# Two DMAs of 64 partitions for one spread row of inverses, in a banded attention with a two-layer network

## The chip, the cores and the metric

The kernel runs on one core of a Trainium2 chip. The metric is device microseconds of one execution, and the median of several runs is compared. The profile is of one execution of its own, whose time stands beside its span below.

## The reference

Banded attention is computed for 8 batches, 8 heads, 576 positions and head dimension 64: each position sees itself and the 63 before it. Its output, 4608 rows of 512, goes through two matrices with a leaky rectifier between them. All is float32.

```python
scores = scale * np.matmul(q, k.transpose(0, 1, 3, 2))
mask = (rel >= 0) & (rel < window)
scores = np.where(mask, scores, -1000000000.0)
scores = scores - np.max(scores, axis=-1, keepdims=True)
attn = np.exp(scores)
attn = attn / (np.sum(attn, axis=-1, keepdims=True) + 1e-09)
out = np.matmul(attn, v)
...
h = x @ w_in
g = np.maximum(0.01 * h, h)
return g @ w_out
```

## The kernel before

**Main work.** The 4608 rows are nine chunks of 512. Chunks 0 to 2 go directly through both matrices: tiles `h` (L431, L919) are the first product and `acc` (L467, L928) the second, each number split into a high and a low part and multiplied three times. Chunks 3 to 8 go two at a time in three passes, in which seven products take the place of eight: `m` (L1117) for the first matrix in all three, `z` (L1180) for the second in the last two; the first pass takes the plain products `y` (L1137) for it. The sums around the products `m` are on VectorE (L1126) and the rectifier on ScalarE (L1129). The weight pieces come through a ring of four tiles that GpSimd fills by DMA (L1101). Pieces of weights that are summed for the seven products are prepared on VectorE and ScalarE (L1032 to L1048) and stored by ScalarE's queue.

**Attention.** It is done in 36 pairs of blocks of 64 queries, ahead of the main work that needs their rows. The first eight pairs, with the main work beside them, follow a list written by hand (`ORDER`). From pair 8 on, a pair m takes these steps, which the change touches in part:

- scores on TensorE (L278), scale and mask on VectorE (L666), from pair 20 on a copy on ScalarE (L672)
- maximum over the keys, which lie on the partitions, on GpSimd (L681), subtraction on VectorE (L688), exponential on ScalarE (L692)
- sum over the keys on GpSimd (L684) into `late_o`, one of two tiles; all partitions hold the same row of 512 sums, one row for each half j of the heads
- compaction: SyncE issues a DMA of one partition's 512 sums to 64 partitions of 8 (L695, `late_c`, one of two tiles); small adds and inverses then take 8 numbers a partition (L699 on ScalarE, L703 on VectorE)
- row store: a DMA of the 1024 inverses to a row of `rows` in device memory (L716)
- spread: a DMA that reads this row back into `late_r` (L728), where partitions 0 to 63 all hold the first 512 numbers and partitions 64 to 127 the other 512. There is one `late_r`, so the spread of a pair waits for the product of the pair before
- values on TensorE (L740), in pairs 8 to 19 a copy on ScalarE (L747, tile `late_n`), and the product with `late_r` on VectorE (L752)
- keep: the result goes to `x_rows` in device memory (L755), and four fetches a pass (L867) bring it back, after which VectorE and ScalarE build the operands of the products `m` (L874, L893, L896)

Pair 19 multiplies by whole sums without compaction and spread, so 27 pairs of the 28 have a spread.

**What sets the order.** From pair 8 on every step is an entry of a plan (`op`, L532), with its engine, its expected duration, the entries that it waits for, a rank, and for DMAs a time to landing. `arrange` (L544) walks the plan as a list scheduler: it takes the engine that can begin first, on it the entry of the lowest rank that is ready, and lets at most eight DMAs of SyncE and ScalarE be under way. Every engine then issues its entries in that order and no other; the waits between engines are semaphores. `load` (L537) makes an entry of SyncE's queue, with a landing time of 4.8 us if none is given; compaction, row store, spread and keep are such entries. The fetch is given 5.0.

Of the kernel before, what the change touches and what calls it, by code (L numbers as in the profile page):

```python
# [104 lines left out]
def band_attention_ffn(ctx: ExitStack, tc: tile.TileContext, qk, vW, vL, w_in, w_out, eye_mask, out, outT):  # L105
    nc = tc.nc
# [298 lines left out]
    later = {}  # L405
# [118 lines left out]
    order, late = ORDER.split("|")  # L524
# [7 lines left out]
    def op(engine, us, fn, *after, rank=1.0, lag=0.12, land=0.0):  # L532
        x = dict(engine=engine, us=us, fn=fn, after=[a for a in after if a], rank=rank, lag=lag, land=land, n=len(plan))
        plan.append(x)
        return x

    def load(fn, *after, rank=1.0, us=0.5, land=4.8):  # L537
        return op("SP", us, fn, *after, rank=rank, land=land)

    def bulk(fn, *after, rank=1.0, land=6.5):  # L540
# [53 lines left out]
    def x_all(k):  # L594
        n = X_FIRST if k < X_FIRST else 7 - X_FIRST
        t = hold("xb", F32R, 2) if k < X_FIRST else hold("few", F32R, FEW)
        return t.rearrange("p (k i c) -> p k i c", k=n, i=2), k - X_FIRST * (k >= X_FIRST)
# [23 lines left out]
    rows = dram.tile([NU // 2, 1024], F32, name="rows")  # L621
# [13 lines left out]
    for name in late.split():  # L635
        kind = name.rstrip("0123456789")
        n = int(name[len(kind) :])
        o = weights_of.setdefault(n, {})
        if kind == "raw":
            o["raw"] = op("ACT", 0.45, partial(fetch_w, n), weights_of.get(n - 3, {}).get("join"), rank=0.2, lag=1.5, land=6.0)  # L640
            continue
        engine, us = ("ACT", ACTS) if kind in ("abs", "chi") else ("DVE", ONE)
        before = {
            "bits": ["raw"], "sign": ["bits"], "abs": ["sign"], "clamp": ["abs"], "join": ["clamp"], "chi": ["join"],
            "rest": ["chi"],
        }[kind]
# [58 lines left out]
    def direct(m):  # L705
        return DIRECT_FROM <= m < EARLY
# [17 lines left out]
    def by_unit(x):  # L724
        return x.rearrange("p (w k c) -> p k w c", k=NP, w=UNITS)

    def spread_of(m):
        nc.sync.dma_start(later["r"], rows[m].rearrange("(j c) -> j c", j=2)[:, None].broadcast_to([2, 64, 512]))  # L728

    def early(m):  # L730
        return m < EARLY
# [37 lines left out]
    at, summing = {}, []  # L769
# [37 lines left out]
    def normalise(m):  # L807

        late = 0.0 if early(m) else 0.45
        soon = 0.15 if early(m) and m > 13 else 0.8 + late  # L810
        o, before, two, after = at[m], at.get(m - 1, {}), at.get(m - 2, {}), at.get(min(m + 2, EARLY - 1))
        if "v" in o and before:
            o["v"]["after"] += [x["V"] for x in (two,) if x]
        if direct(m):
            spread = o["I"] = op("DVE", 4.4, partial(whole_inverse_of, m), o["c0"], o["c1"], rank=soon)
            finish_of(m, [spread], late, soon)
            return
        guard = op("ACT", 0.22, partial(guard_of, m), o["c0"], o["c1"], rank=soon, lag=0.3 + 6 * late)
        o["I"] = op("DVE", 0.25, partial(inverse_of, m), guard, rank=min(0.4 + late, soon))
        o["rows"] = load(partial(rows_of, m), o["I"], rank=0.3 + late)  # L820
        for j in range(2):
            if m + 2 in at and not direct(m + 2):
                at[m + 2][f"c{j}"]["after"].append(o["rows"])
        spread = [load(partial(spread_of, m), o["rows"], before.get("Y"), rank=0.3 + late)]
        finish_of(m, spread, late, soon)

    def finish_of(m, spread, late, soon):
        o, before, two, after = at[m], at.get(m - 1, {}), at.get(m - 2, {}), at.get(min(m + 2, EARLY - 1))
        if early(m):
            free = [after["E1"], before.get("take"), o["A0"] if direct(m) else o["I"]]  # L830
        else:
            free = [both_free if early(m - 2) else two["Y"]]
        o["V"] = op("PE", 1.0, partial(values_of, m), o.get("v"), o["X0"], o["X1"], *free, before.get("V"), rank=0.5 + late, lag=LAG if early(m) else 2 * LAG)
        kept = two.get("kept", [])
        if early(m):
            o["take"] = op("ACT", ACTS, partial(take_of, m), o["V"], *kept, rank=0.5 + late)
        o["Y"] = op("DVE", TWO if early(m) else ONE, partial(product_of, m), *spread, o.get("take"), o["V"], *kept, rank=soon, lag=0.3 + 6 * late)
        for x in summing if direct(m) else ():
            x["after"].append(o["Y"])
        if m < UPC // UNITS * LEAD:  # L840
            hi = op("ACT", ACTS, partial(high_early, m), o["Y"], *x2_free, rank=soon)
            o["kept"] = [op("DVE", TWO, partial(low_early, m), hi, rank=soon)]
            x2.extend(o["kept"])
        else:
            o["kept"] = [load(partial(keep_of, m), o["Y"], rank=0.35 + late)]

# [3 lines left out]
    def x_build(s, n, xt_of, xt_free, x_free):  # L852

        urge, wait = ((0.2, 0.2), (1.4, 2.6), (0.6, 2.6))[s]
        m = (UPC * LEAD + 2 * UPC * s) // UNITS + 2 * n

        def raw():
            return xt_of()[0].rearrange("p (i q c) -> p i q c", i=2, q=4)

        def sums():  # L860
            return xt_of()[1].rearrange("p (k i c) -> p k i c", k=4, i=2)

        def part(q):
            return raw()[:, :, q] if q < 4 else sums()[:, q - 4]

        def fetch():
            nc.sync.dma_start(  # L867
                xt_of()[0].rearrange("p (i c) -> p i c", i=2), x_rows[m : m + 2].rearrange("i p c -> p i c")
            )

        got = [load(fetch, *at[m]["kept"], *at[m + 1]["kept"], *xt_free, rank=urge, land=5.0)]

        def sub(to, a, b):
            nc.vector.tensor_tensor(part(to), part(a), part(b), ALU.subtract)  # L874

        d = op("DVE", 0.5, partial(sub, 4, 0, 2), *got, rank=urge, lag=wait)
        d3 = op("DVE", 0.5, partial(sub, 6, 1, 0), *got, rank=urge, lag=wait)
        d2 = op("DVE", 0.5, partial(sub, 5, 1, 4), d, rank=urge)
        d4 = op("DVE", 0.5, partial(sub, 7, 3, 5), d2, rank=urge)

        def x_view(i, a, b):
            t, k = x_all(a)
            t = t.rearrange("p k i (n c) -> p k i n c", n=4)[:, k : k + b - a, i, n]
            return t.rearrange("p k (i c) -> p k i c", i=2)

        def source(a, b):
            if a < 3:
                return raw()[:, :, 1 + a : 1 + b].rearrange("p i k c -> p k i c")
            return sums()[:, a - 3 : b - 3]

        done = []
        for a, b, after in ((0, 2, got), (2, 3, got), (3, 7, [d, d2, d3, d4])):
            hi = op("ACT", 0.2 + 0.213 * (b - a), lambda a=a, b=b: nc.scalar.copy(x_view(0, a, b), source(a, b)), *after, *x_free, rank=urge, lag=wait)  # L893

            def low(a=a, b=b):
                nc.vector.tensor_tensor(x_view(1, a, b), source(a, b), x_view(0, a, b).bitcast(F32), ALU.subtract)  # L896

            done.append(op("DVE", 0.2 + 0.35 * (b - a), low, hi, rank=urge))
        return done
# [179 lines left out]
    x_free, xt_free = [x for f in range(5) for x in slot_free[f]] + evicted[1], [slot_free[12], slot_free[13]]  # L1079
    x_done = []  # L1080
    for n in range(4):
        xt_free[n % 2] = x_build(0, n, partial(halves_of, XT_AT + n % 2), xt_free[n % 2], x_free)
        x_done += xt_free[n % 2]
# [19 lines left out]
    def filled(of, *after):  # L1103
        n = next(fills)
        return n, op("POOL", 0.6, partial(fill, n, of), *tile_free[n % RING], *after, rank=0.2, land=7.0)
# [97 lines left out]
    def second_in_seven(s):  # L1203
# [70 lines left out]
        if s < NS - 1:  # L1274
            x_done[:] = []
            last_of = {}
            for n in range(4):
                last_of[n % 2] = x_build(s + 1, n, partial(xt_late, n), [*quiet[1], *quiet[2], *last_of.get(n % 2, [])], [x_used])
                x_done.extend(last_of[n % 2])
# [7 lines left out]
    for s in range(NS):  # L1287
        for f in range(half):
# [4 lines left out]
            for k in range(7):  # L1293
                p, b = 7 * f + k, bank_at(s, BANK[k])
                if p % 4 == 0:
                    made_before = [] if s else [y for x in range(f, min(f + 2, half)) for y in prepared[0, x]]
                    n, got = filled(w_first[:, 512 * p : 512 * (p + 4)], *made_before)
                after = bank_free[b] if k < 4 else reads[b]
# [31 lines left out]
        for t in range(2):  # L1330
            for f in range(FT):
                if f % 2 == 0:
                    q = next(pair_of)
                    j, p = f // half, f % half // 2
# [5 lines left out]
                if f % 2 == 0:  # L1340
                    n, got = filled(w_second[:, f : f + 2])
                for i in range(4):
                    after = bank_free[i] if f == 0 else ()
# [9 lines left out]
        if s < NS - 1:  # L1353
            x_done, last_of = [], {}
            for n in range(4):
                tile = 2 * (n % 2)
                free = [split_of[0, f + i * half] for f in (tile, tile + 1) for i in range(2)] + last_of.get(n % 2, [])
                last_of[n % 2] = x_build(s + 1, n, partial(halves_of, tile), free, [x_used])
                x_done += last_of[n % 2]
# [67 lines left out]
```

## Time and profile before

| | before |
|---|---|
| median of 3 runs | 960.24 us (958.60 to 962.86) |
| the profiled execution, its own time | 958.28 us |
| its span, first to last instruction | 956.5 us |
| mean granted TensorE clock | 0.96 |
| TensorE matmul busy | 873.3 us |
| VectorE, ScalarE, GpSimd busy | 609.5, 374.7, 365.3 us |
| DMA traffic | 226.79 MB, mean 237 GB/s |

An instruction's row names its line, engine, operation, output and inputs. In the view of waits a row says which engine, with which tile and line, waited for what: microseconds in total, times, the longest. In the timeline and the chain a row begins with its start and its duration; a bracket gives the idle time ahead of an instruction and what ended it. The view of windows gives for each stretch the busy time of TensorE's matmuls, its weight loads, VectorE, ScalarE and GpSimd with the number of instructions, then the granted clock, the mean busy share of the 16 DMA engines, and GB/s. "SPq" is SyncE's queue, which issues DMAs. A 128x512 matmul group of 336 takes 76.16 us at clock 1.00.

### The profile page before, as it was taken

How to read it: one execution, taken by the hardware profiler on the slowest of the kernel's cores; microseconds unless marked ns; L12 is line 12 of the kernel's file. 1: busy time of each engine (PE TensorE's matmuls, PEld its weight loads, DVE VectorE, ACT ScalarE, POOL GpSimd, SP SyncE). 2: the span in 40 equal slices, each digit the busy share in tenths (PEclk: the TensorE clock that was granted, in tenths of full speed). 3: DMA queues.
4: the chain of work that ended last, by engine and by line, in shares of the span. 5: the costliest groups of instructions: out<-in, count | busy, mean ns of one | idle time of the engine just before them, and what ended most of it. 6: DMA issues, size and time to landing. Idle time of an engine off the chain costs nothing.

```text
span 956.5 us, 16749 instructions
## 1 busy us (share of the span) xinstructions
PE 873.3 (91%) x6778; PEld 704.5 (74%) x6778; DVE 609.5 (64%) x883; ACT 374.7 (39%) x605; POOL 365.3 (38%) x218
## 2 busy tenths in 40 slices
PE   9999999998888799986968799977899999999998
PEld 6877888877767578764857676755688888888886
DVE  7999867455445768554644859537467984455763
ACT  5666553323222344332422324323245442333442
POOL 5321006776756416564736646744011111011110
PEclk9999999999998899997989899978999999999999
DMA  9776758875777669876859697974888787656772
GB/s 331 236 229 191 220 170 269 249 275 190 287 225 252 204 228 327 279 248 204 297 178 350 201 351 256 303 234 136 281 273 225 231 230 227 206 185 185 211 209 99
DMA packets 98531, 226.79 MB, mean 237 GB/s; under 512 B 14743, under 2 KB 45591, under 8 KB 88983
## 3 DMA queue, kind: packets, MB, share of 16 engines
q0 software_dynamic: 23136, 90.18, 30.6%
q10 hardware_dynamic: 35664, 77.31, 24.6%
q1 hardware_dynamic: 39654, 58.24, 18.1%
q8 instruction: 53, 0.87, 0.4%
q14 instruction: 24, 0.19, 0.1%
HBM read 172.52 MB, written 53.06 MB: 236 GB/s over the span
## 4 chain that ended last, share of the span: by engine, by line
PE 49%; DMA 33%; DVE 11%; issue 3%; POOL 2%; ACT 1%; SPq 1%; ACTq 0%; DVEq 0%; POOLq 0%
PE z L1180 16%; PE m L1117 13%; DMA late_r<-rows 12%; DMA late_c<-late_o 7%; PE acc L928 4%; PE h L919 4%; PE h L431 4%; PE acc L467 4%; DMA rows<-late_c 3%; DMA w_second<-p 3%; DMA w_sums<-pspare 2%; PE s L278 1%; DMA w_single<-w 1%; POOL late_o L684 1%; DMA pxb<-sum 1%
## 5 line engine op out<-in xcount | busy, mean ns | idle before, releaser
L1117 PE MATMUL m<-pfew,p 128*128 128x512 f32 x720 | 177.8, 403 | 13.4 <-DVE p L1126 11.2
L1117 PEld LDWEIGHTS m<-pfew,p 128*128 128x128 f32 x720 | 138.9, 195 | 45.2 <-DVE p L1126 12.1
L928 PE MATMUL acc<-p,gs 128*128 128x512 f32 x324 | 81.6, 399 | 0.0
L1129 ACT ACTIVATE p<-p 128x512 f32<-128x512 f32 x60 | 37.8, 631 | 98.5 <-DVE p L1126 98.3
L681 POOL PARTITION_ALL_REDUCE g<-late_f x20 | 38.2, 1938 | 98.9 <-DVE late_f L666 71.3
L1117 PE MATMUL m<-pxb,p 128*128 128x512 f32 x288 | 71.9, 397 | 3.7 <-ACT p L1129 3.4
L1101 POOL DMA_DIRECT2D p<-w_first x42 | 22.7, 541 | 133.5 <-PE m L1117 88.8
L684 POOL PARTITION_ALL_REDUCE late_o<-late_f x20 | 65.0, 3280 | 21.7 <-ACT late_f L692 19.0
L684 POOL PARTITION_ALL_REDUCE late_o<-late_e x18 | 59.8, 3336 | 32.5 <-DMA late_c<-late_o 22.8
L684 POOL PARTITION_ALL_REDUCE late_o<-e x18 | 58.9, 3293 | 33.9 <-ACT e L692 15.5
L928 PEld LDWEIGHTS acc<-p,gs 128*128 128x128 f32 x324 | 60.6, 190 | 13.0
L1126 DVE TENSOR_TENSOR p<-m,pxa 128x512 f32<-128x512 f32 x60 | 41.3, 689 | 41.6 <-PE m L1117 41.3
L1117 PEld LDWEIGHTS m<-pxb,p 128*128 128x128 f32 x288 | 54.5, 191 | 16.4 <-ACT p L1129 3.8
L1137 PE MATMUL y<-gs,p 128*128 128x512 f32 x192 | 50.6, 412 | 12.5 <-DVE p L1126 8.0
L1126 DVE TENSOR_TENSOR pxa<-m,pxa 128x512 f32<-128x512 f32 x60 | 41.3, 688 | 31.1 <-PE m L1117 25.9
L752 DVE TENSOR_TENSOR late_n<-o,late_r 128x512 f32<-128x512 f32 x16 | 10.9, 682 | 76.1 <-DMA late_r<-rows 76.1
L919 PE MATMUL h<-pxa,p 128*128 128x512 f32 x228 | 55.6, 394 | 3.6 <-DVE gs L939 3.6
L1180 PE MATMUL z<-gs,p 128*128 128x512 f32 x240 | 57.7, 390 | 0.0
L1137 PEld LDWEIGHTS y<-gs,p 128*128 128x128 f32 x192 | 37.0, 198 | 22.2 <-DVE p L1126 8.1
L919 PEld LDWEIGHTS h<-pxa,p 128*128 128x128 f32 x228 | 42.9, 190 | 13.8 <-DVE gs L939 4.8
L1180 PEld LDWEIGHTS z<-gs,p 128*128 128x128 f32 x240 | 45.1, 188 | 9.3
L1180 PE MATMUL z<-third,p 128*128 128x512 f32 x216 | 51.9, 390 | 0.0
(191 smaller groups left out, 1778.2 us busy)
## 6 DMA issues: line engine op xcount, KB each, us to landing
p<-w_first POOLq DMA_DIRECT2D x42, 1024.0 KB, 6.8
p<-w_second POOLq DMA_DIRECT2D x28, 1024.0 KB, 7.7
p<-w_sums POOLq DMA_DIRECT2D x16, 1024.0 KB, 5.1
qk<-qk ACTq DMA_DIRECT2D x26, 512.0 KB
pspare<-w_second ACTq DMA_DIRECT2D x16, 512.0 KB
w_sums<-pspare ACTq DMA_DIRECT2D x16, 512.0 KB
raw<-w_out ACTq DMA_DIRECT2D x15, 512.0 KB
raw<-w_in ACTq DMA_DIRECT2D x14, 512.0 KB
```

The lines of the kernel that those rows point to most:

```text
L431: nc.tensor.matmul(ps, a[:, k, :], b[:, k, part], start=n == 0, stop=n == len(terms) - 1)
L467: nc.tensor.matmul(acc[c, i], a[:, ts], b, start=begin and n == 0, stop=end and n == 2)
L681: nc.gpsimd.partition_all_reduce(most_of(j), e_of(m)[:, j], P, ReduceOp.max)
L684: nc.gpsimd.partition_all_reduce(sum_of(j), e_of(m)[:, j], P, ReduceOp.add)
L919: nc.tensor.matmul(ps, a[:, k, :], b[:, k], start=i == 0, stop=i == len(terms) - 1)
L928: nc.tensor.matmul(acc[c, i], a[:, i * P : (i + 1) * P], b, start=begin and k == 0, stop=n in ends and k == 2)
L1101: nc.gpsimd.dma_start(to, of)
L1117: nc.tensor.matmul(tiles[b], w[:, 256 * i + 128 * kt : 256 * i + 128 * kt + 128], x_part(OF_X[k], j, kt), start=begin and c == 0, stop=c = ...
L1126: nc.vector.tensor_tensor(to(), tiles[b], x(), ALU.add)
L1129: nc.scalar.activation(to(), to() if b is None else tiles[b], AF.Prelu, alpha=0.01)
L1137: nc.tensor.matmul(tiles[i], a, b, start=f == 0 and k == 0, stop=f == FT - 1 and k == 2)
L1180: nc.tensor.matmul(tiles[b + i], a, x, start=begin and f == 0 and c == 0, stop=f == half - 1 and c == 2, skip_group_check=not begin,)
```

## The change

The spread becomes two DMAs, one for each 64 partitions, each of which repeats 512 numbers 64 times. The source of the one before had the two halves as its first size and 64 repeats as its second. Three landing times of the plan are other numbers, and the ordered list is made anew from the plan; nothing of the arithmetic changes.

```diff
-    def load(fn, *after, rank=1.0, us=0.5, land=4.8):
+    def load(fn, *after, rank=1.0, us=0.5, land=5.0):
...
-    def spread_of(m):
-        nc.sync.dma_start(later["r"], rows[m].rearrange("(j c) -> j c", j=2)[:, None].broadcast_to([2, 64, 512]))
+    def spread_of(m, j):
+        nc.sync.dma_start(later["r"][64 * j : 64 * j + 64], rows[m, 512 * j : 512 * j + 512][None].broadcast_to([64, 512]))
...
-        spread = [load(partial(spread_of, m), o["rows"], before.get("Y"), rank=0.3 + late)]
+        spread = [load(partial(spread_of, m, j), o["rows"], before.get("Y"), rank=0.3 + late) for j in range(2)]
...
-            o["kept"] = [load(partial(keep_of, m), o["Y"], rank=0.35 + late)]
+            o["kept"] = [load(partial(keep_of, m), o["Y"], rank=0.35 + late, land=6.0)]
...
-        got = [load(fetch, *at[m]["kept"], *at[m + 1]["kept"], *xt_free, rank=urge, land=5.0)]
+        got = [load(fetch, *at[m]["kept"], *at[m + 1]["kept"], *xt_free, rank=urge, land=6.5)]
```

SyncE's queue, in the products `y` of the first pass (in the trace before, this piece begins at 554.68 us). `late_r<-rows` is the spread, `outT` an output store, `x_rows<-late_n` the keep, `late_c<-late_o` a compaction, `rows<-late_c` a row store, `p<-x_rows` a fetch. Before:

```order
L728 DMA late_r<-rows 128x1x512
L1195 DMA outT<-p_25_3083 128x512 x2
L1195 DMA outT<-p_24_2950 128x512 x2
L755 DMA x_rows<-late_n 128x512
L695 DMA late_c_1771<-late_o_1769 64x1x8
L716 DMA rows<-late_c_1772 128x8
L867 DMA p_37_4002<-x_rows 128x2x512
L695 DMA late_c_1771<-late_o_1770 64x1x8
L728 DMA late_r<-rows 128x1x512
```

And in the changed kernel:

```order
L728 DMA late_r<-rows 64x512 x2
L867 DMA p_36_3803<-x_rows 128x2x512
L1195 DMA outT<-p_25_3089 128x512 x2
L1195 DMA outT<-p_24_2972 128x512 x2
L695 DMA late_c_1772<-late_o_1769 64x1x8
L716 DMA rows<-late_c_1771 128x8
L755 DMA x_rows<-late_n 128x512
L695 DMA late_c_1772<-late_o_1770 64x1x8
L728 DMA late_r<-rows 64x512 x2
```

Two spreads stand where one stood, and the row store L716 of the next pair, which had stood behind the keep L755 of this one, now stands ahead of it.

TensorE's queue, in the products `m` of the second pass, around the values of the last pair (`o<-late_f,more_v`, L740). Each row of six matmuls is one of the seven products of a group, and `m_3_2` is a tile of group 3; a group has four tiles, three of which take two products. Before:

```order
L1117 MATMUL m_3_0_5988<-pxb_3408,p_32_3607 128x512 x6
L1117 MATMUL m_3_1_5998<-pfew_3418,p_32_3607 128x512 x6
L1117 MATMUL m_3_2_6007<-pfew_3418,p_32_3607 128x512 x6
L740 MATMUL o_6017<-late_f,more_v 64x64 x16
L1117 MATMUL m_3_3_6036<-pfew_3418,p_29_3487 128x512 x6
L1117 MATMUL m_3_0_5988<-pfew_3418,p_29_3487 128x512 x6
```

And in the changed kernel:

```order
L1117 MATMUL m_3_3_6033<-pxb_3413,p_29_3490 128x512 x6
L1117 MATMUL m_4_0_6072<-pxb_3413,p_30_3529 128x512 x6
L1117 MATMUL m_4_1_6083<-pfew_3422,p_30_3529 128x512 x6
L740 MATMUL o_6094<-late_f,more_v 64x64 x16
L1117 MATMUL m_4_2_6113<-pfew_3422,p_30_3529 128x512 x6
L1117 MATMUL m_4_3_6125<-pfew_3422,p_30_3529 128x512 x6
```

The values of the last pair stood between the third and the fourth product of group 3, and now stand between the second and the third of group 4, six products of six matmuls later.

## The prediction

> **What bounds the kernel now.** The page comes first.
>
> ```profile
> PE 873.3 (91%) x6778; PEld 704.5 (74%) x6778; DVE 609.5 (64%) x883; ACT 374.7 (39%) x605; POOL 365.3 (38%) x218
> ```
>
> TensorE is the busy engine, but a share over the whole span hides stages. The view of windows, cut where the work changes, gives for each stretch its length, the busy time of each engine, the granted clock, the DMA share and GB/s:
>
> ```profile
> 173.00:337.00 164.00, 143.47 (x1430) 114.53 (x1431) 86.24 (x126) 52.23 (x98) 99.31 (x40) 0.94 0.71 236
> 337.00:409.00 72.00, 67.38 (x582) 54.52 (x581) 48.35 (x72) 29.79 (x52) 32.99 (x20) 1.00 0.82 276
> 409.00:693.00 284.00, 233.45 (x2012) 186.21 (x2012) 166.11 (x218) 93.23 (x154) 152.65 (x87) 0.90 0.78 255
> 693.00:956.50 263.50, 259.43 (x1144) 214.29 (x1142) 168.31 (x196) 104.25 (x133) 27.81 (x44) 1.00 0.70 208
> ```
>
> The last stage is full: 259.43 of 263.50 us busy at clock 1.00. The loss lies in the stretches where attention pairs run beside the main products. In 409 to 693 TensorE idles 284.00 - 233.45 = 50.6 us, and what it does runs at a mean clock of 0.90. As a rough estimate of its work at full clock I take 233.45 x 0.90 = 210 us, so this stage loses 74 us. By the same sum 173 to 337 holds 143.47 x 0.94 = 135 us of work and loses 29 us, and 337 to 409 loses under 5.
>
> Next, who TensorE waits for; first in 409 to 693 (total, times, longest):
>
> ```profile
> PE o L740 <- DVE late_n L752: 15.2, 3, 7.7
> PE m L1117 <- DVE p L1126: 11.5, 3, 9.1
> PE y L1137 <- DVE p L1126: 8.0, 1, 8.0
> PE o L740 <- DMA more_v<-vL: 7.8, 1, 7.8
> ```
>
> L752 is the product of a pair with `late_r`, the spread row of inverses. L1126 is an ordinary sum of the main work. Why should that be late? The timeline around 450 us shows it (start, duration, idle before and its releaser):
>
> ```profile
> 449.75 0.69 DVE L752 TENSOR_TENSOR late_n<-o,late_r 128x512 f32<-128x512 f32 x1 [11.77 <-DMA late_r<-rows]
> 450.03 0.21 ACT L699 ACTIVATE late_c<-late_c 128x8 f32<-128x8 f32 x1 [11.39 <-DMA late_c<-late_o]
> 450.20 3.23 POOL L684 PARTITION_ALL_REDUCE late_o<-e  x1 [9.49 <-DMA late_c<-late_o]
> 450.36 0.68 DVE L1126 TENSOR_TENSOR p<-m,pxa 128x512 f32<-128x512 f32 x1
> ...
> 451.09 1.22 PE L1117 MATMUL m<-pfew,p 128*128 128x512 f32 x2 [9.05 <-DVE p L1126]
> ```
>
> VectorE stands at L752 for 11.77 us, the sum L1126 queues behind it, and TensorE waits 9.05 us for a sum that has nothing to do with attention. ScalarE and GpSimd stand in the same microsecond for `late_c<-late_o`, a transfer of 2 KB issued just after the spread. How fast is the spread? The chain of waits in 409 to 693, its first and last such piece of six (start, duration):
>
> ```profile
> 412.70 15.54 DMA late_r<-rows
> ...
> 632.51 17.74 DMA late_r<-rows
> ```
>
> The six sum to 104.8 us, 17.5 each, for 256 KB. What the DMA engines do meanwhile, by windows, in the tail of one spread and in a busy stretch:
>
> ```profile
> 445.00:449.00 4.00, 0.00 (x0) 0.00 (x0) 0.00 (x0) 0.00 (x0) 0.00 (x0) 0.66 0.16 58
> ...
> 560.00:570.00 10.00, 10.00 (x98) 7.99 (x98) 4.30 (x4) 1.23 (x3) 7.38 (x3) 0.88 1.05 353
> ```
>
> From 445 to 449 no compute engine works at all, and the DMA share is 0.16: 0.16 x 16 is about 2.6 engines, where the other stretch fills all 16. So the spread trickles through two or three engines, with the others empty.
>
> This is also a loop. There is one `late_r`, so the spread of pair m waits for the product of pair m-1. One turn is the spread 17.5, its product 0.69 and the issue 0.54, or 18.7 us; 15 products lie in the 284 us, one each 18.9. The stage runs at the pace of the spread. TensorE's 210 us of work would need one in 14.0.
>
> **The change, part by part.** *The transfer.* Its source had two as its first size; each half now has 64, its partitions, on both sides. That the engines used follow the first size is my reading of the 0.16; no row of this trace varies that size alone. The Trainium skill, page "DMA: Bandwidth & Descriptors", section "Rules for kernel authors", says that an outermost size below 16, a broadcast of few copies above all, confines a DMA to at most that many engines; the 0.16 agrees. By that rule the halves go over all engines, and the sum below stays as it is.
>
> What do the two halves take together? No row shows this read over all engines, so I bound it by the nearest: large loads (KB each, median us to landing), and one 256 KB transfer of the chain that shared its queue with a slow spread.
>
> ```profile
> p<-w_first POOLq DMA_DIRECT2D x42, 1024.0 KB, 6.8
> p<-w_second POOLq DMA_DIRECT2D x28, 1024.0 KB, 7.7
> p<-w_sums POOLq DMA_DIRECT2D x16, 1024.0 KB, 5.1
> ```
>
> ```profile
> 301.14 11.69 DMA x_rows<-late_n
> ```
>
> So 5.1 us, or somewhat less, since those move four times the bytes, up to 11.7. I take 6, next to the loads. A turn of the loop is then 6 + 0.69 + two issues of 0.54, about 7.8 us, and even at 11.7 it is 13.5, under the 14.0 that TensorE needs. The loop stops being the bound in either case.
>
> *The added issues.* SyncE issues 27 more transfers:
>
> ```profile
> L728 SPq DMA_DIRECT2D late_r<-rows x27: 526/541/613, 173.8 to 690.4; - x27
> SPq L755 <- DVE late_n L752: 98.8, 12, 17.1
> ```
>
> 27 x 0.54 = 14.6 us on a queue that stood 98.8 us in 409 to 693 alone, waiting at L755 for that product. While it stands there the next row store, compactions and spread are queued behind it. This wait hides the issues; without that cover they cost 15 x 0.54 = 8 us in the loop.
>
> *The list made anew.* The three landing figures are the planner's (spread, compaction and row store 5.0, keep 6.0, fetch 6.5) and move instructions on all engines. What they move at the places above: SyncE issues a row store ahead of the keep that waits for a product where it had it behind, and the values of the last pair stand six products of six matmuls later. The first takes a wait out of the pair's chain; the second gives each pair more TensorE time. Against a faster transfer I cost both at nothing beyond what is kept back below: what they could cost is the time of a stall that stays.
>
> *The sum*, against the profiled execution (span 956.5, time 958.28). In 409 to 693: the waits on the spread, 15.2 + 11.5 + 8.0 = 34.7 us, go. So does the 7.8 on `more_v`, whose issuing engine, ScalarE, is the one that stands at L699 for the 2 KB transfers. That is 42.5 of 50.6 us idle, 84%; with the same share of the 23.4 us lost to the clock (20) it is 62. What is late next? The stage moves
>
> ```profile
> DMA packets 29067, 72.53 MB, mean 255 GB/s; under 512 B 5940, under 2 KB 12084, under 8 KB 24756
> 555.00:628.00 73.00, 59.86 (x562) 46.40 (x560) 47.06 (x56) 24.75 (x40) 45.44 (x25) 0.95 0.87 286
> ```
>
> and in 222 us that would be 327 GB/s, between the 286 of its busiest long stretch and the 353 above. I keep 15 us back for transfers that then collide: 72.53 MB at 306 GB/s is 237 us, a gain of 47. In 173 to 337 the waits are indirect:
>
> ```profile
> PE s L278 <- ACT late_n L747: 6.0, 2, 3.2
> PE h L919 <- DVE gs L939: 5.9, 4, 2.3
> PE o L740 <- DVE late_e L666: 5.1, 2, 4.7
> ```
>
> VectorE's wait for the spread, in 173 to 409 and then in 409 to 693:
>
> ```profile
> DVE late_n L752 <- DMA late_r<-rows: 46.4, 8, 7.1
> ```
>
> ```profile
> DVE late_n L752 <- DMA late_r<-rows: 76.1, 8, 12.7
> ```
>
> In the earlier stretch it is 46.4 us, and what is behind it is what TensorE waits for; but the pairs follow closer there and GpSimd is 99.31 of 164 us busy. I take half of 29 or a little more, 16. The other stretches give 2. Together 47 + 16 + 2 = 65: 893.3 as a profiled time. The median of the runs shown, 960.24, is 2.0 above the profiled one, so **895 us**.
>
> **The rivals.** *Transfers become the bound.* If the DMA engines hold 409 to 693 to the 286 GB/s of its busiest long stretch, it takes 72.53 / 0.286 = 254 us, a gain of 30; with 10 from the earlier stage that is about 920. For it: shares of 0.87 already. Against: 353 GB/s in one stretch.
>
> *Nearly everything goes.* If 10 us of loss stay in 409 to 693, 8 in 173 to 337 and 5 elsewhere, the gain is 64 + 21 + 4 = 89: 871. For it: the last stage loses only 4 of 263.5. Against: small waits on VectorE and ScalarE remain.
>
> *The halves are no faster: slower.* Each half reads one 2 KB row 64 times; if what makes the spread slow is that read, or if the halves go one behind the other on the same engines, the pair lands in 17.5 us as before and the loop only gains an issue, 15 x 0.54 = 8 us: 968. It decides from a landing of about 12.2 us, where the turn passes 14.0, and is a loss from 17.5 on. Against it: the 0.16, which says idle engines and no slow memory. A rule of the Trainium skill stands with it, same page and section: two transfers to disjoint halves of the partitions aren't worth it, since they serialize over the same engines, and one of 128 partitions is better. By this rule the time is that 968. The trace can't refute it for halves, but the rule takes a transfer over all engines for the alternative, which 0.16 doesn't show here.
>
> *The spread is faster and TensorE doesn't profit*, since the remade list puts other waits in its place: 958 to 963. Against: the last stages are full in the list as it is.
>
> **How the numbers follow.** About 0.5% (4.8 us) is what a measurement of this kernel can tell from no change. Forecast (880 to 908) 0.50; nearly everything (858 to 880) 0.19; transfers the bound (908 to 935) 0.22; no faster halves 0.05; no profit 0.04. Faster is the first three, 0.91; same 0.04; slower 0.05. The range leaves out the low end of the second case, the upper part of the third and the last two: 866 to 930.
>
> **What would show it.** In the changed profile `late_r<-rows` lands in 5 to 9 us, and VectorE's wait for it in 409 to 693, now 76.1 us, falls below 20; the chain of waits there loses most of its 104.8 us of spreads; ScalarE's and GpSimd's waits for `late_c` shrink with it; the mean clock of the stage rises from 0.90 toward 0.97, and its GB/s to about 300. If the landing stays above 12 us, the reading of the 0.16 was wrong. If it falls and TensorE still idles over 30 us there, the step that fails is that the spread alone set the pace.

## The result, and the profile after

The changed kernel takes 866.82 us (median of 4 runs, 866.17 to 867.62) where the one before takes 959.42; the ratio is 0.9032, with an interval of 0.9003 to 0.9061. The forecast was 895, the range 866 to 930: the direction and the mechanism came out, the gain was 93 us and not 65, and the time lies 0.8 us inside the low end of the range. That it lies inside is in part luck: on another chip the same kernel took 864.63 us, just below the range.

The profiled execution took 867.03 us, its span is 865.2. Its page:

```profile
PE 848.2 (98%) x6778; PEld 688.3 (80%) x6778; DVE 623.6 (72%) x883; ACT 376.8 (44%) x605; POOL 368.0 (43%) x218
...
PE 81%; DMA 7%; DVE 6%; issue 2%; POOL 2%; ACT 1%; ACTq 0%; SPq 0%; POOLq 0%; DVEq 0%
```

TensorE was busy 91% of the span and is now busy 98%; the second line is the chain of work that ended last, 81% of which is TensorE itself. By windows, cut where the same work begins (the first group of the products `m` at 370.4 us before and 339.9 after, the first products `z`, those of the second pass, at 723.9 and 632.8). Before, from the products `m` to there:

```profile
370.00:724.00 354.00, 299.99 (x2532) 240.49 (x2531) 211.19 (x283) 119.61 (x198) 178.77 (x104) 0.92 0.80 261
```

And after, the early pairs first:

```profile
173.00:307.00 134.00, 134.00 (x1431) 108.13 (x1431) 100.84 (x127) 52.31 (x96) 101.61 (x40) 1.00 0.87 290
307.00:340.00 33.00, 33.00 (x264) 27.05 (x263) 27.68 (x40) 15.95 (x27) 12.85 (x8) 1.00 0.81 278
340.00:633.00 293.00, 283.29 (x2466) 229.34 (x2465) 203.17 (x277) 120.40 (x198) 176.46 (x103) 0.98 0.95 312
633.00:865.20 232.20, 228.44 (x1008) 188.88 (x1006) 151.20 (x170) 93.10 (x115) 24.42 (x39) 1.00 0.66 199
```

Up to 370.4 or 339.9 us 30.5 us came; from there to 723.9 or 632.8, 60.6; behind that 0.2. The two make 91.1 of the 91.3 us between the spans. In the early stretch from 173 us, which took 164 us, TensorE now works without a gap, at clock 1.00. VectorE's wait for the spread and the landings of spread and compaction, in the views of these two tiles (us, times; then min, median, max from issue to landing):

```profile
  DMA late_r<-rows: 1.6, 2
...
DMA to landing us min/median/max: 3.6/6.0/8.6
```

```profile
DMA to landing us min/median/max: 1.6/5.2/11.1
```

The wait fell from 122.5 us in all (46.4 and 76.1 in the two stretches of the prediction) to 1.6. The compactions, for which ScalarE and GpSimd had stood 11 and 9 us in one place, land in 5.2 us by the median.

### The profile page after: what moved, and what is told of

Its sections match the earlier page's. It is cut to its first block, busy times and chain, and to the rows that moved or that the text cites. A ratio compares the mean times of both kernels' runs of the same rounds, so it can differ in the third digit from the quotient of the medians.

```text
span 865.2 us, 16790 instructions
## 1 busy us (share of the span) xinstructions
PE 848.2 (98%) x6778; PEld 688.3 (80%) x6778; DVE 623.6 (72%) x883; ACT 376.8 (44%) x605; POOL 368.0 (43%) x218
## 4 chain that ended last, share of the span: by engine, by line
PE 81%; DMA 7%; DVE 6%; issue 2%; POOL 2%; ACT 1%; ACTq 0%; SPq 0%; POOLq 0%; DVEq 0%
PE m L1117 26%; PE z L1180 18%; PE acc L928 10%; PE h L919 10%; PE h L431 5%; PE acc L467 4%; PE s L278 3%; DMA rows<-late_c 3%; PE o L740 3%; DMA late_r<-rows 2%; POOL late_o L684 1%; DMA w_sums<-pspare 1%; DMA raw<-w_out 1%; PE o L367 1%; DVE pspare L1035 1%
## 5 line engine op out<-in xcount | busy, mean ns | idle before, releaser
L1117 PE MATMUL m<-pfew,p 128*128 128x512 f32 x720 | 170.7, 393 | 0.0
L1117 PEld LDWEIGHTS m<-pfew,p 128*128 128x128 f32 x720 | 135.5, 189 | 28.7
L1180 PE MATMUL z<-pxa,p 128*128 128x512 f32 x216 | 51.9, 389 | 0.0
L1137 PE MATMUL y<-gs,p 128*128 128x512 f32 x192 | 47.4, 399 | 4.3 <-ACT pxa L1162 2.8
L1137 PE MATMUL y<-pxa,p 128*128 128x512 f32 x192 | 47.3, 395 | 1.8 <-DVE pxa L1166 1.8
```

Of the source, the lines that this page charges most:

```text
L1117: nc.tensor.matmul(tiles[b], w[:, 256 * i + 128 * kt : 256 * i + 128 * kt + 128], x_part(OF_X[k], j, kt), start=begin and c == 0, stop=c = ...
L1137: nc.tensor.matmul(tiles[i], a, b, start=f == 0 and k == 0, stop=f == FT - 1 and k == 2)
L1180: nc.tensor.matmul(tiles[b + i], a, x, start=begin and f == 0 and c == 0, stop=f == half - 1 and c == 2, skip_group_check=not begin,)
```

## The experiments

**The transfer without the list.** In the kernel before, the one entry of the plan issues both halves, so that the order on every engine is that of before and only the transfer differs:

```diff
-        nc.sync.dma_start(later["r"], rows[m].rearrange("(j c) -> j c", j=2)[:, None].broadcast_to([2, 64, 512]))
+        [nc.sync.dma_start(later["r"][64 * j : 64 * j + 64], rows[m, 512 * j : 512 * j + 512][None].broadcast_to([64, 512])) for j in range(2)]
```

> The two halves are issued by one entry of the plan, so that every engine's order is that of before; only the transfer is new. Theory (the narrow transfer alone set the pace, and the old list was planned for a landing of 4.8 us that the halves come near): the spread lands in about 6 us as in the changed kernel, VectorE's wait for it falls from 122.5 us below 15, and the time is 870 to 890 us, that is at least four fifths of the 92.6 us gained. Rival (the remade list carries a good part of the gain): 905 to 935 us.

871.60 us, against 959.97 on the same chip: ratio 0.9067 (0.9029 to 0.9104). That is 88 of the 93 us. VectorE's wait for the spread, in its view:

```profile
  DMA late_r<-rows: 3.5, 4
...
DMA to landing us min/median/max: 2.7/5.5/12.3
```

The theory holds; the rival, that the list carries a good part, falls.

**The list without the transfer.** The other corner: the changed kernel's list, the old DMA.

```diff
+        if j == 0:
+            nc.sync.dma_start(later["r"], rows[m].rearrange("(j c) -> j c", j=2)[:, None].broadcast_to([2, 64, 512]))
```

> The list of the changed kernel, where the first of its two entries issues the one DMA of the old form and the second issues nothing. Theory: the spread takes about 17 us again, the loop of one spread and one product sets the pace, and the time is 945 to 985 us. Rival (the list carries a good part): 900 to 930 us.

951.58 us, ratio 0.9908 (0.9875 to 0.9941): 8 us of gain, under 1%. VectorE waits again:

```profile
  DMA late_r<-rows: 101.7, 17
```

So the remade list is worth something under the slow transfer, about 8 us, and under the fast one no gain is shown: there the lists of before and of the changed kernel give 0.9067 and 0.9032, with intervals that overlap.

**Two DMAs with two as their first size.** Is it the number of DMAs, or their shape? Here each of the two takes half of the columns for all partitions:

```diff
-        nc.sync.dma_start(later["r"][64 * j : 64 * j + 64], rows[m, 512 * j : 512 * j + 512][None].broadcast_to([64, 512]))
+        columns = slice(256 * j, 256 * j + 256)
+        nc.sync.dma_start(
+            later["r"][:, columns],
+            rows[m].rearrange("(j c) -> j c", j=2)[:, columns][:, None].broadcast_to([2, 64, 256]),
+        )
```

> The list of the changed kernel and two DMAs a spread, but each takes half of the columns for all 128 partitions, so that the source of each has two as its first size. Theory (what counts is the first size, which leaves most DMA engines idle): each pair of DMAs takes as long as the one of before or a little longer, since its pieces are 1 KB, and the time is 945 to 1000 us. Rival (two DMAs are faster than one because they go side by side, whatever their shape): a landing below 10 us and 866 to 890 us.

966.88 us, ratio 1.0059 (1.0028 to 1.0089), with 89.2 us of VectorE's wait for the spread. Two DMAs by themselves bring nothing; it is the shape. One more thing differs: the pieces are 1 KB here, and 2 KB in the halves of the changed kernel. The next two runs both have pieces of 2 KB.

**62 and 2 partitions, and 32 and 32.** Is it a large first size that helps, or its divisors?

```diff
+        for n, k in ((64 * j, 62), (64 * j + 62, 64 - 62)):
+            nc.sync.dma_start(later["r"][n : n + k], rows[m, 512 * j : 512 * j + 512][None].broadcast_to([k, 512]))
```

> The changed kernel with each half cut into 62 and 2 partitions. If any large first size spreads a DMA over all engines, 62 does, the parts of 2 move only 4 KB, and the time is 866 to 880 us. The Trainium skill, page DMA: Bandwidth & Descriptors, section on why a DMA increments its semaphore by 16, says that the engines used are the largest number up to 16 that divides the first sizes, which for 62 is 2: by this rule the spread is as slow as before and the time is 940 to 990 us.

> The control for the cut at 62: each half cut into 32 and 32 partitions, so as many DMAs, with a first size that 16 divides. Both theories: the landing stays near 6 us and the time at 866 to 880 us; the two added issues of about 0.5 us a pair are hidden. Rival (the number of DMAs on SyncE's queue matters): 885 us or more.

966.01 us (ratio 1.0088, 1.0053 to 1.0123) for 62 and 2, 873.71 us (0.9104, 0.9054 to 0.9154) for 32 and 32. The views of `late_r`, of 62 and 2 first, then of 32 and 32:

```profile
  DMA late_r<-rows: 93.4, 21
```

```profile
  DMA late_r<-rows: 6.1, 4
...
DMA to landing us min/median/max: 2.1/5.0/8.7
```

With as many DMAs and the same bytes, one cut is as slow as the kernel before. The rule of the Trainium skill, page "DMA: Bandwidth & Descriptors", section "Why a DMA increments its semaphore by 16 and not by 1", that the engines used are the largest number up to 16 that divides the first sizes, is what these two times agree with: 2 for 62, 16 for 32 and 64. A rule by size alone doesn't fit them. The DMA packets that the two traces record for SyncE's queue (a packet is one piece that one DMA engine moves) show the width itself. From 441.4 to 449.7 us in the one with 62, while a spread is under way, at most two packets of 2 KB run at once in 99% of the time; from 429.0 to 431.5 us in the one with 32, up to 17 do. The parts of 2 partitions are narrow by either rule; they move 4 KB each, and what they add was not measured by itself.

**A narrow DMA that nobody waits for.** The prediction gave two harms: VectorE waits for the product's operand, and other transfers wait behind the spread. To have the second without the first, the changed kernel gets one more DMA of the old form behind each pair of halves, to a place in device memory that nothing reads; the control has one of the same bytes with 64 as its first size. The two differ in this:

```diff
-            nc.sync.dma_start(spare_rows[m], rows[m].rearrange("(j c) -> j c", j=2)[:, None].broadcast_to([2, 64, 512]))
+            nc.sync.dma_start(spare_rows[m], rows[m][None].broadcast_to([64, 1024]))
```

> The changed kernel, with one more DMA behind each pair of halves: the narrow form of before (two as its first size, 256 KB), to a place in device memory that nobody reads, so that no product waits for it. Theory A (the narrow transfer costs by the wait of the one product and its single buffer): 867 to 880 us. Theory B (it costs as much by what it does to others: the compactions, row stores and halves behind it share its two or three engines and its place in the queue): the compactions take over 12 us again, and the time is 905 us or more.

> The control for the idle narrow DMA: the changed kernel with one more DMA of 256 KB behind each pair of halves, to a place that nobody reads, but with 64 as its first size on both sides. It has the same bytes, the same number of DMAs and the same issues. Theory (the narrowness did the harm): 867 to 885 us. Rival (another 7 MB and 27 transfers in the middle of a stage whose DMA share is 0.95 did it, or their places among the eight DMAs under way): 920 us or more.

The narrow one: 978.46 us, ratio 1.0184 (1.0123 to 1.0245), so all of the gain is lost and a little more. The wide one: 873.68 us, 0.9119 (0.9074 to 0.9165). The narrow one lies 112 us above the 866.82 of the changed kernel, which ran on another chip; the wide one lies 9 above the 864.63 of the changed kernel on the same chip. The bytes and the number of DMAs are the same. The pieces are not, 4 KB in the wide one and 2 KB in the narrow one; but the halves of the spread have pieces of 2 KB as well, and they are fast. With the narrow one VectorE's wait for the spread stays short, in the view of `late_r`:

```profile
  DMA late_r<-rows: 5.3, 2
```

What is long is the waits for the compactions (ScalarE, GpSimd), and SyncE's for the row store, the compactions and the idle DMA itself. In the views of waits, of all engines and of SyncE's queue:

```profile
ACT late_c L700 <- DMA late_c<-late_o: 45.8, 5, 14.3
...
POOL late_o L685 <- DMA late_c<-late_o: 28.3, 4, 11.3
```

```profile
SPq L729 <- DMA rows<-late_c: 60.4, 17, 9.6
...
SPq L717 <- DMA late_c<-late_o: 45.3, 7, 12.5
...
SPq L696 <- DMA spare_rows<-rows: 30.0, 5, 6.9
```

The transfers of 2 KB that are issued behind a narrow one come late: ScalarE stands up to 14.3 us for one, where its longest such wait in the wide control is 2.8. Theory B holds: the narrow transfer need not be waited for to do as much harm as the whole gain. SyncE waits for the idle DMA itself (L696, 30.0 us) although nothing reads it, so part of the harm may come through SyncE's issues and not through the engines that the transfers share; the two parts weren't separated. In the wide control the landings are as in the changed kernel (KB each, median us):

```profile
late_r<-rows SPq DMA_DIRECT2D x54, 128.0 KB, 5.9
spare_rows<-rows SPq DMA_DIRECT2D x27, 256.0 KB, 5.8
```

**The planner's figures.** The changed kernel's plan with the figures of before, on two chips, and with only keep and fetch set back; on the second chip the changed kernel itself stands beside them. All three figures set back:

```diff
-    def load(fn, *after, rank=1.0, us=0.5, land=5.0):
+    def load(fn, *after, rank=1.0, us=0.5, land=4.8):
...
-            o["kept"] = [load(partial(keep_of, m), o["Y"], rank=0.35 + late, land=6.0)]
+            o["kept"] = [load(partial(keep_of, m), o["Y"], rank=0.35 + late)]
...
-        got = [load(fetch, *at[m]["kept"], *at[m + 1]["kept"], *xt_free, rank=urge, land=6.5)]
+        got = [load(fetch, *at[m]["kept"], *at[m + 1]["kept"], *xt_free, rank=urge, land=5.0)]
```

> The changed kernel with the planner's three landing figures as before (4.8 for all, 5.0 for the fetch), so that the list is made anew by other numbers. Theory (the figures are a small matter against the transfer): 866 to 876 us, with TensorE's idle time in the middle of the span below 20 us. Rival (the figures matter, since a list planned too tight stalls behind each late landing): 880 us or more.

> The changed kernel as it is, for a comparison on one chip with the two that follow: 864 to 870 us.

> The list made by the planner's figures of before (4.8 for all, 5.0 for the fetch), against the changed kernel on one chip. If these figures give a better list it is 3 to 6 us faster than the changed kernel; if what was seen was scatter between chips, it is within 2 us of it.

> The figures for keep and fetch as before (5.0 here for the keep by the default, 5.0 for the fetch), the default of 5.0 left in. If the longer figures for these two cost the few microseconds, it comes out with the list of old figures, 860 to 864 us; if the default does, with the changed kernel, 865 to 869 us.

The first gave 862.80 us, 0.8972 (0.8936 to 0.9008), 4 us better than the changed kernel had been. On the second chip the changed kernel took 864.63 us (0.9046, 0.9007 to 0.9085), the old figures 866.76 (0.9049, 0.9008 to 0.9090), keep and fetch alone set back 872.05 (0.9115, 0.9078 to 0.9151). The old figures come out 2.1 us behind the changed kernel, so the 4 us did not return. The third list is some 7 us slower, and the guess for it, 860 to 869, was wrong; intervals of it and of the changed kernel touch, and why this list would be worse stays open. No version was found that beats the changed kernel beyond the scatter.

## Why the prediction was right, and where its sizes were off

**The narrow transfer.** The reading of the share of 0.16 as two or three engines at work was right: a first size of two gives the slow time in one DMA and in two, and 62 gives it as well. The rival of halves that are no faster, at 968, falls: with two halves the kernel takes 0.9032 of its time. The prediction set beside it the rule of the Trainium skill (same page, "Rules for kernel authors") that two transfers to disjoint halves aren't worth it. That rule compares with one transfer over all 16 engines, which the one here was not, so it doesn't lead to 968 and these runs don't decide on it; a single DMA of 128 partitions as wide as the halves wasn't tried.

One thing was missed. The spread had even these two engines only in part. From 446 to 448 us, in the trace before, the packets of all queues together take the time of 2.0 engines: 1.30 for 8 KB packets of GpSimd's queue, 0.48 for 4 KB packets of ScalarE's, and only 0.24 for the spread's 2 KB packets. One of these takes 0.08 to 0.10 us, so 128 of them on two engines and nothing else would need some 6 us (an estimate). On this reading the 17.5 us come from two engines and from sharing them with the other queues, whose last packets run as late as the spread's.

**The landing.** 6 us was taken, from bounds of 5.1 and 11.7; the median of a half, from its own issue, is 6.0, with 3.6 and 8.6 as ends. Within bounds that wide, meeting it so closely is in part luck.

**The loop of one buffer.** The arithmetic fitted, 18.7 us a turn and a product each 18.9, and it goes with the spread. But it was named as what set the pace, and the narrow DMA that nobody waits for shows it isn't needed for that. There the last 16 products with the spread begin one each 21.3 us (from 410.4 to 730.3), although VectorE waits only 5.3 us in all for the spread; before it was one each 19.3 (from 411.6 to 701.5), and in the changed kernel one each 16.8. What a narrow transfer does to the rest, which the prediction took for an accompaniment, is enough to take all of the gain. In that run it shows as waits of ScalarE and GpSimd for 2 KB and of SyncE for row stores. Those of ScalarE and GpSimd are in the kernel before as well, in the view of waits:

```profile
ACT late_c L699 <- DMA late_c<-late_o: 40.0, 5, 11.4
...
POOL late_o L684 <- DMA late_c<-late_o: 32.8, 6, 10.3
```

How the 93 us divide between the loop and these other waits isn't shown.

**The two sizes that were off.** Of the loss of 29 us in the early stretch only half was taken to go, because GpSimd was busy 99.31 of 164 us. All of it went: GpSimd is busy 101.61 of 134 us and TensorE all of 134, so GpSimd didn't bind. Up to the products `m` 30.5 us came, where the sum had 16 and part of the 2. (The three rows of TensorE's waits that the prediction gives for 173 to 337 are those of 173 to 409; in 173 to 337 alone `h` has 4.7 us and not 5.9. The sum doesn't use them.) The other is the 15 us kept back for transfers that collide. From the products `m` to the first products `z` 60.6 us came, where the sum had 47 and part of the 2. That is near the 62 that it had before the 15 were kept back. The step failed as a reading of the DMA share: the stage now runs at a share of 0.95 and 312 GB/s, as the sum had it (306), but TensorE idles for only 10 of its 293 us. Its longest waits in the whole span:

```profile
PE m L1117 <- ACT p L1129: 3.7, 1, 3.7
PE y L1137 <- ACT pxa L1162: 2.8, 1, 2.8
```

No DMA is among them, and the rest of the rows are 1.8 us or less each. The rival of transfers that become the bound (920) fell with it, and the one of nearly everything gone (871) is what happened. Both sizes were kept down in the same way: the high share of busy time of a resource, GpSimd's in one stretch and the DMA engines' in the other, was taken as a reason that the work that waits for it would be late.

**The list.** It was costed at nothing beside the faster transfer, and the two corners show 88 us for the transfer alone, 8 for the list alone and 93 for both.

**The signs that were named.** Landing 5 to 9 us: median 6.0. VectorE's wait below 20: 1.6 in the whole span. The chain of waits, which lost most of its 104.8 us of spreads: 17.7 are left from 340 to 633. The waits of ScalarE and GpSimd for `late_c`: 40.0 and 32.8 us in all before, 0.3 and none after. The mean clock of the stage toward 0.97: 0.98 in 340 to 633. About 300 GB/s: 312.

## What to carry to other kernels

Look at the first size of both sides of every DMA, the broadcast of a row above all: here 128 partitions that were written as two times 64 had about two engines, and so had 62 partitions. Then look at the DMA share in a stretch in which the compute engines stand still: a low share beside a wait for a transfer, 0.16 here, is a sign that the transfer is narrow and not that the memory is slow. And ask of a slow transfer not only who waits for it, but what is issued behind it on its queue: here engines stood up to 14.3 us for 2 KB.

## What the runs showed of the hardware

A narrow transfer of 256 KB behind each of 27 spreads, which nothing reads, cost some 110 us, about 100 more than one of the same bytes with 64 as its first size. While a narrow spread was under way, its packets took turns with those of other queues on about two engines, and 256 KB took 17.5 us where the idle wide 256 KB landed in 5.8. And a DMA share of 0.95 at 312 GB/s over 293 us in the changed kernel, and 0.96 at 323 GB/s in the wide control, went with TensorE busy 283.29 and 281.32 of the 293 us. The stretch in the wide control:

```profile
340.00:633.00 293.00, 281.32 (x2491) 227.47 (x2482) 203.96 (x275) 118.83 (x197) 175.66 (x103) 0.98 0.96 323
```
